# Attention into routed experts on one core: load pieces, second buffers, and the work between the two phases

## The chip, the core and the metric

The kernel runs on one core of a Trainium2 chip. The core has TensorE (PE in the profile; its weight loads are PEld), VectorE (DVE), ScalarE (ACT), GpSimd (POOL) and SyncE (SP, which here only issues transfers), and 16 DMA engines that all queues share. The metric is the device time of one execution in microseconds (us). Three runs of the kernel before took 674.9, 676.65 and 677.34 us.

## The reference, cut to what matters

The output of a decayed attention without softmax is the input of a mixture of eight experts, in which every token goes to exactly one expert and every expert takes exactly 576 of the 4608 tokens.

```python
scores = q @ k.T / sqrt(64)                       # 8 batches, 8 heads, 576 positions, 64 dims
ret = (scores * where(rel >= 0, gamma[h] ** rel, 0)) @ v
x = ret.transpose(0, 2, 1, 3).reshape(4608, 512)
flat = (x @ w_gate).flatten()                     # 4608 x 8 logits
for idx in argsort(-flat):                        # greedy: best pair first
    tok, e = idx // 8, idx % 8
    if assigned[tok] < 0 and counts[e] < 576: assigned[tok] = e; counts[e] += 1
for e in range(8):
    out[assigned == e] = relu(x[assigned == e] @ w1[e]) @ w2[e]     # 512 -> 1024 -> 512
```

## The kernel before

**Attention.** The work is cut into 16 units (4 pairs of batches times 4 pairs of heads) of 9 blocks of 128 positions. A unit needs four tiles from memory: `kin` and `qin` (transposed, 128 x 1152), `vin` (128 x 1152) and `nin` (k in rows, 128 x 1024). GpSimd scales `nin` to `ks` (`kscale2`, L568). On TensorE `A` makes the products k times q (L588), which VectorE multiplies by the decay into `am` (L593). `ST` sums the running state (L605, ScalarE scales it at L611). `XS` and `XW` add state and block parts into `pX` (L630, L640), which VectorE scales into `xT` (`scale`, L652). The constants of the decay lie in the tile `cst`, a part for each pair of heads. The loads of units 0 and 1 come in pieces (`pieces`, L549, in the order of the string that `fetch` gets). Those of later units are whole tiles (`load`, L529), issued two units ahead. `kin`, `qin` and `vin` have three buffers, `nin` has one. All go out on SyncE's queue, and each tracked transfer there waits for the one eight issues earlier.

**Rows and logits.** Every four units complete a pair of batches. `logits` and `logits2` compute its logits (L669, L682), and `rows` transposes it on VectorE into the tile `xr` (L693, one buffer, three blocks to a tile), from where four transfers (L698) write it to the table `xd` in memory. The last pair's nine blocks go over TensorE: `rows_pe` turns a block by a transpose (L711) or by a product with the identity (L709), ScalarE copies it (L715) and a transfer writes it (L716). These small pieces are also used to fill TensorE's waits in the first search (`idle`).

**Routing.** The greedy choice is a search for a threshold, digit by digit. `first_digits` cuts the ordered logits into five digits, `first_table` compares them with all digit values on VectorE, `first_table_slow` does it for columns 24 to 31 on GpSimd (L202), and `count_first_pe` counts the first digit on TensorE (L241). `search_first` then goes through the digits: a product with ones (L258) broadcasts the result, VectorE finds the digit `j` (L260) and the candidates (L268), TensorE counts them with the next table (L290) and adds the carried count (L291). `members` and `listing` turn the threshold into the 576 token numbers `idx` of expert 0.

**Experts.** `gather` fetches an expert's rows from `xd` with five indirect transfers (L953), and `transposes` turns them (L969) and splits them into a high part `xh` and a low part `xl` (L971, L972). Weights come in eight chunks of 512 KB to an expert (L923, four buffers `raw`). `conv` splits a chunk into high and low: two ScalarE copies (L937, L941), and an accumulating transfer on GpSimd's queue (L942) that gives the low part; only the first chunk's low part is made by VectorE (L939). `l1` makes 16 groups of 12 products (L998), each followed by a ReLU on ScalarE (L1002), `l2` the second layer (L1037), and `scatter` writes the rows. The search for the next expert runs on VectorE beside them. A model of time (`Mixer`) decides, when the program is built, between which products its steps stand; on the chip every engine runs its list in order.

`warm` issues products of a constant tile (L1114) whose result nobody reads.

Of the kernel before, what the change touches and what calls it, by code (L numbers as in the profile page):

```python
# [23 lines left out]
def consts_np():  # L24
# [16 lines left out]
    f = lambda a: np.ascontiguousarray(a, dtype=np.float32).reshape(128, -1)  # L41
    return np.concatenate([f(m1), f(m2), f(np.stack([e1, e1, e2], axis=2)), f(ks), f(ss)], axis=1)

# [38 lines left out]
class Route:  # L82
# [14 lines left out]
    def setup(s):  # L97
# [16 lines left out]

        s.DF, s.inc, s.sm, s.oz, s.D1 = T("DF", [5, 36], BF16), T("inc", [5], I32), T("sm", [2, 5], I32), T("oe", [43, 8], BF16), T("D1", [36], F32)
        s.oe = s.oz[:, 7:]
# [7 lines left out]
        o = [256]  # L124
# [44 lines left out]
    def first_digits(s, c0, c1):  # L169

        V = s.nc.vector
        yield from s.ordered(c0, c1)
        n = c1 - c0
        d, o = s.dg[:, :5, c0:c1], s.om[:, 1:2, c0:c1].to_broadcast([128, 5, n])
        for x, op in ((o, ALU.logical_shift_right), (d, ALU.bitwise_and)):
            V.tensor_tensor(d, x, s.sm[:, op == ALU.bitwise_and, :, None].to_broadcast([128, 5, n]), op=op)
            yield
        if c1 > 24:
            V.tensor_copy(s.D1[:, c0:c1], d[:, 1])
        V.tensor_tensor(s.DF[:, :, c0:c1], d, s.inc[:, :, None].to_broadcast([128, 5, n]), op=ALU.add)  # L180
        yield
        V.tensor_tensor(s.D2[:, :, c0:c1], d[:, 2:, :, None].to_broadcast([128, 3, n, 2]),
                        s.inc[:, 2:, None, None].to_broadcast([128, 3, n, 2]), op=ALU.add)
        yield

    def first_table(s, i, g0, g1):
        n, k = g1 - g0, widths(FIRST)[i]
        if k == 64:
# [7 lines left out]
                                  op=ALU.is_le)  # L196

    def first_table_slow(s, i, c0, c1):

        for c in range(c0, c1):  # L200
            k = widths(FIRST)[i]
            s.nc.gpsimd.tensor_scalar(s.FT[i][:, c//4, :, c % 4], s.kt[:, :k, 0], s.D1[:, c:c+1], None, op0=ALU.is_le)  # L202

# [45 lines left out]
    def search_first(s):  # L249
# [4 lines left out]
        f, cp, v, oh = s.f0, s.cp0, s.DF[:, 0], s.oh  # L254
        yield 300, 30
        for i, K in enumerate(KK):
            jp = ps.tile([128, 8], F32, name="r")
# [14 lines left out]
            oh = s.oe  # L272
            t = pool.tile([128, 36], F32, name="vl")
# [3 lines left out]
            if i == 0 and len(s.pending) > 3:  # L277
                s.pending.pop(0)()
            if s.pending:
# [6 lines left out]
            for n, (a, b) in enumerate(pieces):  # L286
                yield 200, 25*(b - a)
                for c in range(a, b, w):
                    st = s.FT[i+1][:, c:c+2].rearrange("p c k -> p (c k)") if w == 2 else s.FT[i+1][:, c//4, :, c % 4]
                    nc.tensor.matmul(cw, st, s.oz[:, c+w-1:c+w+7].rearrange("p c e -> p (c e)"), start=(c == 0), stop=False, skip_group_check=True)  # L290
            nc.tensor.matmul(cw[:, 64-8*w:72-8*w], sel.to_broadcast([128, 128]), cp, start=False, stop=True, skip_group_check=True)  # L291
            if w == 1:
# [86 lines left out]
    def members(s, p):  # L379
# [24 lines left out]
        if not p:  # L404
            s.idle("rows")
            s.idle(2)
        yield (3000 if 0 < p < E - 1 else 1550 if not p else 1900), 125
# [8 lines left out]
    def listing(s, p):  # L416
# [25 lines left out]
        if not p:  # L442
            s.idle("rows")
            s.idle(6)
        for g0, g1 in ((0, 9),) if p else ((0, 5), (5, 9)):
# [62 lines left out]
def attention(tc, nc, P, qk, vk, cst_d, wg_d, rf, xd, Lg):  # L508
    cst = P['c'].tile([128, 2*1024+3*512+64+16], F32, name="cst", tag="xg")
    W0 = cst.shape[1]  # L510
    m1 = cst[:, 0:1024].rearrange("p (h q) -> p h q", h=8)
    m2 = cst[:, 1024:2048].rearrange("p (h q) -> p h q", h=8)
    ex = cst[:, 2048:3584].rearrange("p (h j q) -> p h j q", h=4, j=3)
    ks = cst[:, 3584:3648].rearrange("p (h q) -> p h q", h=4)
    ss = cst[:, 3648:3664].rearrange("p (h q) -> p h q", h=4)
    wg = P['a'].tile([128, HP, 32], F32, name="wg")
    LD = {}
    def load(u, what, cuts=None):

        bp, hp = divmod(u, HP)  # L520
        for i in what:
            n = 1024 if i == "n" else 1152
            t = P['ld'].tile([128, n], F32, name=i + "in", bufs=dict(q=3, k=3, v=3, n=1)[i])
            src = qk[bp, hp, "qk".index(i)] if i in "qk" else vk[bp, hp, :, :1152] if i == "v" else vk[bp, hp, :, 1152:]
# [9 lines left out]
    def consts(hp):  # L534
        for a, n in ((0, 256), (2048, 384), (1024, 256)):
            if a or hp:
                part(a + n*hp, a + n*hp + n)
    load(0, "kqvn", (256, 512))
    load(1, "kqvn", (512,))

    def fetch(order):
        for x in order.split():
            if x == "c":
                part(0, 256)
                part(3584, 3664)
# [27 lines left out]
    def A(g):  # L573
# [15 lines left out]
        if j == n - 1:  # L589
            m = m2 if tail else m1  # L590
            for h in range(2):
                am = P['w'].tile([128, n, 128], F32, name=f"am{h}" + tail, bufs=2)
                nc.vector.tensor_tensor(am, PA[0][h], m[:, None, 2*hp+h, :].to_broadcast([128, n, 128]), op=ALU.mult)  # L593
                for i in range(n): AM[g-j+i, h] = am[:, i]
# [105 lines left out]

    def rows_pe(bp, blk, product=False, hps=range(HP)):

# [40 lines left out]
    for bp in range(NP):  # L743
        g0 = (bp+1)*4*NB + 2
        for k, b0 in enumerate((0, 3, 6)):
# [11 lines left out]
            else:  # L757
# [3 lines left out]
                else:  # L761
                    at(G-1, lambda it: rest(both(it, R.first_digits(27, 30))), it)
        if bp < NP-1:
# [69 lines left out]
    bp = NP-1  # L833
    left = [lambda b=b: rows_pe(bp, b, b > 0) for b in range(NB)]

# [17 lines left out]
    some(1)  # L853
    return R, [lambda b=b, h=h: rows_pe(bp, b, True, h) for b in range(NB - len(left), NB) for h in [(x,) for x in range(HP)]]

# [31 lines left out]
def moe(tc, nc, P, R, xd, w1_d, w2_d, out, mix):  # L887
# [8 lines left out]
    spacer = P['c'].tile([1, 1], F32, name="spacer")  # L896

# [78 lines left out]
    def l1(e, tr):  # L976
# [5 lines left out]
        for i, (f, s) in enumerate(order):  # L982
# [88 lines left out]
    def run():  # L1071
# [5 lines left out]
        mix.step()  # L1077
        warm(20)
        mix.adv(3500)
        tr = transposes(0)  # L1080
        next(tr)
        warm(3)
# [9 lines left out]
def build(tc, nc, qk, vk, cst, wg, rf, w1, w2, out):  # L1092
    with ExitStack() as top:
# [4 lines left out]
        top.enter_context(tc.manual_schedule())  # L1098
        xd = dr.tile([N, DM], F32, name="xd")
        it = P['c'].tile([128, 128], I32, name="it")  # L1100
        nc.gpsimd.iota(it, pattern=[[1, 128]], base=0, channel_multiplier=-1)
# [4 lines left out]
        mix = Mixer()  # L1106
        full = P['c'].tile([128, 512], BF16, name="full")
        nc.vector.memset(full, 1.0)

# [6 lines left out]
        with ExitStack() as ctx:  # L1116
# [5 lines left out]
            def idle(what):  # L1122

                if what not in ("row", "rows"):
                    warm(what)
                    return
                for _ in range(1 + (what == "rows")):
                    if rows:
                        rows.pop(0)()
                    else:  # L1130
                        warm(1)
            R.idle = idle
            run = moe(tc, nc, P, R, xd, w1, w2, out, mix)
# [23 lines left out]
```

## Time and profile before

| what | value |
|---|---|
| three runs | 674.9, 676.65, 677.34 us |
| the profiled execution: own time, span | 674.55 us, 672.8 us |
| TensorE busy | 632.0 us, 94% of the span |
| VectorE, ScalarE, GpSimd busy | 422.3, 273.6, 180.7 us |
| moved by DMA | 134.72 MB, mean 200 GB/s |
| idle TensorE up to 240 us, where attention, routing and the first layer of expert 0 lie | 27.8 us |

The span is cut into stages by time: the attention's units run up to about 174 us, the last rows and the first search up to 198 us, the gathers of expert 0 up to 207 us, and the experts from there to the end. A row of the timeline gives an instruction's start, its duration and, in brackets, how long its engine was idle before it and what it waited for. One float32 product shows as two instructions on TensorE.

### The profile page before, as it was taken

The numbers are of one execution on the slowest core, as the hardware profiler recorded it, in microseconds if no ns is written. First come the engines' busy times: TensorE is split into PE (matmuls) and PEld (weight loads), VectorE is DVE, ScalarE is ACT, GpSimd is POOL, SyncE is SP. The second block draws the span as 40 slices with busy tenths as digits, with TensorE's granted clock in tenths as the row PEclk, the third lists the DMA queues.
The fourth block names the chain that finished last, engine by engine and source line by source line (L and its number), as shares of the span: only waits on it lengthen the run. The fifth ranks groups of instructions, "written<-read, shape, count | busy, mean of one in ns | idle before, by whom it ended". The sixth has DMA issues, their size and how long they took to land.

```text
span 672.8 us, 14118 instructions
## 1 busy us (share of the span) xinstructions
PE 632.0 (94%) x5376; PEld 543.3 (81%) x5376; DVE 422.3 (63%) x1603; ACT 273.6 (41%) x488; POOL 180.7 (27%) x234
## 2 busy tenths in 40 slices
PE   4999999897987999999999999999999999999995
PEld 3887788776756887797798799889889989988984
DVE  2477878777775797798799599679776302211200
ACT  1333333232325524655257245515724643652611
POOL 2222212212212106315214323315224134131111
PEclk9999999899998999999999999999999999999998
DMA  7997999993455946978859938947894895894421
GB/s 225 340 362 251 285 306 307 257 282 91 126 198 137 227 96 203 258 192 199 247 130 230 243 81 215 245 145 172 210 245 118 177 268 177 194 237 137 94 63 39
DMA packets 53427, 134.72 MB, mean 200 GB/s; under 512 B 6128, under 2 KB 22512, under 8 KB 53360
## 3 DMA queue, kind: packets, MB, share of 16 engines
q1 hardware_dynamic: 38400, 81.91, 37.1%
q0 software_dynamic: 14960, 51.91, 35.1%
q8 instruction: 42, 0.69, 0.4%
q14 instruction: 25, 0.20, 0.1%
HBM read 81.90 MB, written 18.87 MB: 150 GB/s over the span
## 4 chain that ended last, share of the span: by engine, by line
PE 63%; DVE 12%; issue 9%; DMA 8%; POOL 3%; ACT 3%; SPq 2%; POOLq 0%; DVEq 0%; ACTq 0%
PE py L1037 21%; PE ph L998 21%; PE pX L640 4%; PE pA L588 3%; PE pX L630 3%; PE pS L605 3%; DMA w2l<-raw 2%; DMA raw<-in_w 1%; POOL xg L953 1%; DMA qin<-in_qk 1%; PE pt L969 1%; PE r L340 1%; DMA xd<-xr 1%; PE pT L669 1%; DVE xr L693 1%
## 5 line engine op out<-in xcount | busy, mean ns | idle before, releaser
L1037 PE MATMUL py<-w2h,hb 128*128 128x512 f32 x576 | 188.3, 399 | 0.0
L998 PE MATMUL ph<-xh,w1h 128*128 128x320 f32 (+1 forms) x512 | 152.6, 302 | 2.5 <-ACT xh L971 1.7
L998 PE MATMUL ph<-xh,w1l 128*128 128x320 f32 (+1 forms) x512 | 150.0, 297 | 0.0
L998 PE MATMUL ph<-xl,w1h 128*128 128x320 f32 (+1 forms) x512 | 149.9, 297 | 0.0
L1037 PE MATMUL py<-w2l,hb 128*128 128x512 f32 (+1 forms) x320 | 125.4, 392 | 0.1
L1037 PEld LDWEIGHTS py<-w2h,hb 128*128 128x128 f32 x576 | 104.0, 188 | 20.7
L998 PEld LDWEIGHTS ph<-xh,w1h 128*128 128x128 f32 x512 | 96.7, 190 | 4.7 <-ACT xh L971 2.8
L998 PEld LDWEIGHTS ph<-xl,w1h 128*128 128x128 f32 x512 | 96.9, 191 | 0.5 <-DVE cs L344 0.3
L998 PEld LDWEIGHTS ph<-xh,w1l 128*128 128x128 f32 x512 | 96.7, 191 | 0.2 <-DMA w1l<-raw 0.2
L1005 DVE SCALAR_TENSOR_TENSOR hb<-ph,hb 128x256 fp32r<-128x256 f32 (+1 forms) x192 | 58.9, 351 | 56.9 <-ACT hb L1002 56.2
L1002 ACT ACTIVATE hb<-ph 128x256 fp32r<-128x256 f32 (+1 forms) x128 | 52.2, 409 | 102.1 <-PE ph L998 102.1
L611 ACT ACTIVATE S<-pS,cst 64x128 f32<-64x128 f32 x128 | 46.4, 363 | 108.1 <-PE pS L605 106.5
L1014 POOL DMA_INDIRECT out_y<-yt,idx x40 | 40.8, 1021 | 118.8 <-ACT yt L1054 76.6
L1037 PEld LDWEIGHTS py<-w2l,hb 128*128 128x128 f32 (+1 forms) x320 | 56.7, 177 | 13.7 <-DMA w2l<-raw 1.0
L568 POOL TENSOR_TENSOR ks<-nin,cst 128x512 f32<-128x512 f32 (+1 forms) x33 | 33.3, 1028 | 120.8 <-DMA nin<-in_vk 100.9
L1054 ACT ACTIVATE yt<-py 128x512 f32<-128x512 f32 x32 | 19.2, 599 | 105.1 <-PE py L1037 78.9
L942 POOL DMA_DIRECT2D w2l<-raw x32 | 28.8, 901 | 119.2 <-ACT hb L1002 119.2
L593 DVE TENSOR_TENSOR am<-pA,cst 128x512 f32<-128x512 f32 x64 | 41.0, 682 | 27.9 <-PE pA L588 21.8
L953 POOL DMA_INDIRECT xg<-xd,idx x40 | 40.7, 1017 | 51.6 <-issue 26.6
L1057 DVE TENSOR_TENSOR yt<-yt,py 64x512 f32<-64x512 f32 x8 | 5.4, 678 | 69.6 <-ACT yt L1056 69.4
L588 PE MATMUL pA<-qin,kin 64*128 64x128 f32 x512 | 39.5, 295 | 8.6 <-DMA qin<-in_qk 8.6
L588 PEld LDWEIGHTS pA<-qin,kin 64*128 64x128 f32 x512 | 33.0, 196 | 12.8 <-issue 8.0
(190 smaller groups left out, 967.8 us busy)
## 6 DMA issues: line engine op xcount, KB each, us to landing
raw<-in_w SPq DMA_DIRECT2D x64, 512.0 KB, 5.3
w2l<-raw POOLq DMA_DIRECT2D x32, 512.0 KB, 5.7
w1l<-raw POOLq DMA_DIRECT2D x31, 512.0 KB, 7.7
kin<-in_qk SPq DMA_DIRECT2D x14, 576.0 KB, 6.3
qin<-in_qk SPq DMA_DIRECT2D x14, 576.0 KB, 7.1
vin<-in_vk SPq DMA_DIRECT2D x14, 576.0 KB, 7.9
nin<-in_vk SPq DMA_DIRECT2D x14, 512.0 KB, 5.8
xd<-xr SPq DMA_DIRECT2D x36, 192.0 KB, 3.6
```

Source lines behind the costliest of these rows:

```text
L568: nc.gpsimd.tensor_tensor(KS[u][:, a:b], LD[u, 'n'].rearrange("p (a d) -> p a d", d=64)[:, a:b], ks[:, u % HP, a:b, None].to_broadcast([12 ...
L588: nc.tensor.matmul(PA[0][h][:, j], LD[u, 'k'][r, s], LD[u, 'q'][r, s], start=True, stop=True, skip_group_check=True)
L593: nc.vector.tensor_tensor(am, PA[0][h], m[:, None, 2*hp+h, :].to_broadcast([128, n, 128]), op=ALU.mult)
L611: nc.scalar.activation(st[64*h:64*h+64, :, 64*h:64*h+64], PS[u][64*h:64*h+64], AF.Copy, scale=ss[64*h:64*h+64, hp, c:c+1])
L640: nc.tensor.matmul(px[64*h:64*h+64, :], v[:, blk*128+64*h:blk*128+64*h+64], AM[g, h], start=False, stop=blk < 8, skip_group_check=True)
L942: nc.gpsimd.dma_start(lo, raw, accum_op=ALU.add)
L953: nc.gpsimd.indirect_dma_start(out=xg[:n, j, :], out_offset=None, in_=xd[:, :], in_offset=bass.IndirectOffsetOnAxis(ap=found[e][:n, j:j+1] ...
L998: T.matmul(ps, w, x, start=(k == 0), stop=(k == 11))
L1002: A.activation(hb[:, f, c], ps, AF.Relu)
L1005: V.scalar_tensor_tensor(hb[:, f, to+a:to+b], ps[:, a:b], 0.0, hb[:, f, 256*s+a:256*s+b].bitcast(F32), op0=ALU.max, op1=ALU.subtract)
L1014: st = nc.gpsimd.indirect_dma_start(out=out[:, :], out_offset=bass.IndirectOffsetOnAxis(ap=found[e][:n, t:t+1], axis=0), in_=y[:n], in_off ...
L1037: T.matmul(ps[:m], a, w, start=(k == 0), stop=(k == last), skip_group_check=True)
```

## The change

It has four parts.

1. **Start of the attention.** The constants are laid out so that each pair of heads takes one transfer instead of three. The first pieces of unit 0 are 512 columns instead of 256 and all pieces of units 0 and 1 are issued at once; the first `qin` piece goes out on ScalarE's queue. Seven `warm` products precede the first four blocks of `A`.
2. **Second buffers.** `nin` and `xr` get two buffers.
3. **Digits and rows.** Columns 24 to 27 and 28 to 35 of the second digit's table are made by VectorE, and the six last columns get their digits in one pass. All last rows are turned by transposes, in half blocks. The carried count is added between the two parts of a count, not behind it.
4. **Late weights.** Only two chunks of expert 0 are requested before the gathers. A transfer of one element, which waits for the fourth gather, stands in SyncE's queue ahead of the others. The conversions of the first layer move to other groups, and there are more `warm` products.

On SyncE's queue the program begins as follows, before and then after (k, q, v, n are the four tiles, `cst` the constants):

```order
L549 DMA kin<-in_qk 128x256
L549 DMA qin<-in_qk 128x256
L532 DMA cst<-in_cst 128x256
L532 DMA cst<-in_cst 128x80
L549 DMA vin<-in_vk 128x256
L549 DMA nin<-in_vk 128x256
L549 DMA kin<-in_qk 128x256
L549 DMA qin<-in_qk 128x256
L532 DMA cst<-in_cst 128x384
L532 DMA cst<-in_cst 128x256
L549 DMA nin<-in_vk 128x256
L549 DMA vin<-in_vk 128x256
```

```order
L537 DMA kin<-in_qk 128x512
L523 DMA cst<-in_cst 128x336
L537 DMA nin<-in_vk 128x512
L537 DMA vin<-in_vk 128x512
L537 DMA kin<-in_qk 128x640
L537 DMA qin<-in_qk 128x640
L523 DMA cst<-in_cst 128x640
L537 DMA nin<-in_vk 128x512
L537 DMA vin<-in_vk 128x640
```

Unit 0 and its constants took sixteen transfers, of which the first twelve stand here. Now they take nine on this queue, and the first `qin` piece has left it.

On VectorE these rows stand between the last count of the first digit and the first search step (`om`, `dg`, `DF`, `D` are the digits' steps, `f` and `cp` the first digit's result, `j` the digit found), before and then after:

```order
L180 TENSOR_TENSOR DF<-dg,inc 128x5x3
L182 TENSOR_TENSOR D_496<-dg,inc 128x3x6
L246 TENSOR_TENSOR f_2301<-cnt,room_478 128x8
L247 TENSOR_TENSOR cp_2302<-cnt,room_478 128x8
L155 TENSOR_SCALAR om<-m 128x3
L157 TENSOR_TENSOR om<-m,om 128x3
L176 TENSOR_TENSOR dg<-om,sm 128x5x3
L176 TENSOR_TENSOR dg<-dg,sm 128x5x3
L179 CAST D_495<-dg 128x3
L180 TENSOR_TENSOR DF<-dg,inc 128x5x3
L182 TENSOR_TENSOR D_496<-dg,inc 128x3x6
L260 TENSOR_REDUCE j<-r 128x1
```

```order
L223 TENSOR_TENSOR G_2264<-rc_f,m 128x384
L214 TENSOR_TENSOR oh<-t_476,mx_477 128x24
L156 TENSOR_SCALAR om<-m 128x6
L158 TENSOR_TENSOR om<-m,om 128x6
L239 TENSOR_TENSOR f_2284<-cnt,room_473 128x8
L240 TENSOR_TENSOR cp_2285<-cnt,room_473 128x8
L177 TENSOR_TENSOR dg<-om,sm 128x5x6
L177 TENSOR_TENSOR dg<-dg,sm 128x5x6
L179 TENSOR_TENSOR DF<-dg,inc 128x5x6
L181 TENSOR_TENSOR D_490<-dg,inc 128x3x12
L254 TENSOR_REDUCE j<-r 128x1
```

The digits of the last six columns, which were made in two passes of seven instructions, are made in one of six.

On SyncE's queue the last row of `xd` is followed by the weights of expert 0 (`raw`), before and then after:

```order
L716 DMA xd_65<-xT_2239 128x512
L923 ISA
L923 DMA raw_2554<-in_w1 128x1024
L923 ISA
L923 DMA raw_2556<-in_w1 128x1024
L923 ISA
L923 DMA raw_2558<-in_w1 128x1024
```

```order
L701 DMA xd_65<-xT_2231 128x512
L905 ISA
L905 DMA raw_2551<-in_w1 128x1024
L905 ISA
L905 DMA raw_2553<-in_w1 128x1024
L1069 DMA spacer1_2293<-xg_2611 1x1
L905 ISA
L905 DMA raw_2695<-in_w1 128x1024
```

Behind the second chunk now stands a transfer that reads the gathered rows `xg`. On TensorE the order of all products of the experts is the one of before, and so it is on VectorE.

The diff, without the renamed lines and the `warm` counts:

```diff
-        if c1 > 24:
-            V.tensor_copy(s.D1[:, c0:c1], d[:, 1])
...
-    def first_table_slow(s, i, c0, c1):
-
-        for c in range(c0, c1):
-            k = widths(FIRST)[i]
-            s.nc.gpsimd.tensor_scalar(s.FT[i][:, c//4, :, c % 4], s.kt[:, :k, 0], s.D1[:, c:c+1], None, op0=ALU.is_le)
...
                 for c in range(a, b, w):
-                    nc.tensor.matmul(cw, st, s.oz[:, c+w-1:c+w+7].rearrange("p c e -> p (c e)"), start=(c == 0), stop=False, skip_group_check=True)
-            nc.tensor.matmul(cw[:, 64-8*w:72-8*w], sel.to_broadcast([128, 128]), cp, start=False, stop=True, skip_group_check=True)
+                    nc.tensor.matmul(cw, st, s.oz[:, c+w-1:c+w+7].rearrange("p c e -> p (c e)"), start=(c == 0), stop=(c + w == 36), skip_group_check=True)
+                if n == 0:
+                    nc.tensor.matmul(cw[:, 64-8*w:72-8*w], sel.to_broadcast([128, 128]), cp, start=False, stop=False, skip_group_check=True)
...
-            t = P['ld'].tile([128, n], F32, name=i + "in", bufs=dict(q=3, k=3, v=3, n=1)[i])
+            t = P['ld'].tile([128, n], F32, name=i + "in", bufs=dict(q=3, k=3, v=3, n=2)[i])
...
     def consts(hp):
-        for a, n in ((0, 256), (2048, 384), (1024, 256)):
-            if a or hp:
-                part(a + n*hp, a + n*hp + n)
-    load(0, "kqvn", (256, 512))
+        part(80 + 896*hp + (0 if hp else 256), 976 + 896*hp)
+    load(0, "kqvn", (512,))
...
-                part(0, 256)
-                part(3584, 3664)
+                part(0, 336)
...
-                nc.sync.dma_start(*pieces[x[0].isupper(), x[0].lower()].pop(0))
-    fetch("k0 q0 c v0 n0 k1 q1 h0 n1 v1 k2 q2 n2 v2")
+                (nc.scalar if x == "q0" else nc.sync).dma_start(*pieces[x[0].isupper(), x[0].lower()].pop(0))
+    fetch("k0 q0 c n0 v0 k1 q1 h0 n1 v1 K0 Q0 h1 N0 V0 K1 Q1 N1 V1")
...
-            TR[0] = P['w'].tile([128, 12, HP, 32], F32, name="xr", bufs=1)
+            TR[0] = P['w'].tile([128, 12, HP, 32], F32, name="xr", bufs=2)
...
-            if product:
-                nc.tensor.matmul(o, x, ident, start=True, stop=True)
-            else:
-                nc.tensor.transpose(o, x, ident)
+            nc.tensor.transpose(o, x, ident)
...
-    kscale2(0, 0, 4)
-    A(0)
-    A(1)
+    kscale2(0, 0, 8)
+    P['warm'](7)
+    for g in range(4):
+        A(g)
     ST(0, 0)
-    kscale2(0, 4, 8)
     kscale2(0, 8, 16)
-    fetch("K0 Q0 N0 V0 h1 K1 Q1 N1 V1")
-    A(2)
-    A(3)
...
-    R.first_table_slow(1, 24, 28)
-    b = R.first_digits(30, 33)
+    R.first_table(1, 6, 7)
     logits2(bp, 6, 9)
     some(3)
-    rest(both(R.count_first(33, 36), b))
-    R.first_table_slow(1, 28, 32)
-    c = R.first_digits(33, 36)
+    P['warm'](2)
+    rest(R.count_first(33, 36))
+    c = R.first_digits(30, 36)
+    for _ in range(2):
+        next(c)
     R.count_first_pe([27, 30, 33], **tag())
     rest(c)
-    R.pending = [lambda: R.first_table(1, 8, 9)] + [lambda i=i: R.first_table(i, 6, 9) for i in (2, 3, 4)]
+    R.pending = [lambda: R.first_table(1, 7, 9)] + [lambda i=i: R.first_table(i, 6, 9) for i in (2, 3, 4)]
...
-    state = dict(dma=0, conv=0, most=4, listing=-1)
+    state = dict(dma=0, conv=0, most=2, listing=-1)
...
-            if s and f in (1, 2, 4, 6) or e == 0 and i < 3:
+            if s and f in (1, 2, 4, 6) or e == 0 and i in (0, 2, 4):
                 conv()
...
         mix.adv(800)
+
+        nc.sync.dma_start(spacer2, XG[0][0:1, 3, 0:1])
         state['most'] = 8*E
+        dma_pump()
```

## Rows read from the trace of the kernel before

**Rows 1.** Windows of the start: us busy per engine (instructions), PEclk, DMA share, GB/s

```profile
2.20:28.36 26.16, 17.79 (x200) 15.52 (x201) 8.18 (x16) 6.36 (x15) 4.50 (x6) 1.00 0.88 291
14.00:16.00 2.00, 2.00 (x16) 1.75 (x12) 1.31 (x3) 0.00 (x0) 0.41 (x2) 1.00 0.40 117
16.00:28.00 12.00, 11.26 (x154) 9.89 (x152) 5.58 (x12) 4.17 (x12) 2.09 (x2) 1.00 0.95 339
36.00:46.00 10.00, 9.75 (x148) 8.49 (x146) 7.07 (x38) 3.81 (x12) 2.05 (x2) 1.00 1.03 373
```

**Rows 2.** Timeline of the start, TensorE: start, us, instruction, idle before and releaser

```profile
12.62 2.08 PE L588 MATMUL pA<-qin,kin 64*128 64x128 f32 x16 [3.56 <-DMA qin<-in_qk]
...
28.36 1.16 PE L588 MATMUL pA<-qin,kin 64*128 64x128 f32 x16 [1.02 <-DMA qin<-in_qk]
```

**Rows 3.** Waits of TensorE from 0 to 240: total us, times, longest

```profile
PE pA L588 <- DMA qin<-in_qk: 8.6, 4, 3.6
PE pX L630 <- DVE xT L652: 6.8, 4, 2.8
```

**Rows 4.** Timeline of the attention's last units, VectorE and TensorE

```profile
150.55 0.71 DVE L693 STREAM_TRANSPOSE xr<-xT 128x512 f32<-128x512 f32 x1 [1.35 <-DMA xd<-xr]
...
152.32 0.49 PE L630 MATMUL pX<-qin,S 128*128 128x128 f32 x2 [1.39 <-DVE xT L652]
...
162.68 0.71 DVE L693 STREAM_TRANSPOSE xr<-xT 128x512 f32<-128x512 f32 x1 [2.02 <-DMA xd<-xr]
...
164.22 0.49 PE L630 MATMUL pX<-qin,S 128*128 128x128 f32 x2 [2.75 <-DVE xT L652]
```

**Rows 5.** Windows behind these stalls

```profile
152.00:158.00 6.00, 5.56 (x80) 4.88 (x82) 5.22 (x16) 1.61 (x5) 2.04 (x2) 1.00 0.22 83
164.00:170.00 6.00, 5.77 (x65) 4.24 (x65) 4.89 (x12) 2.18 (x6) 0.00 (x0) 0.72 0.08 15
```

**Rows 6.** Timeline from the last logits to the third digit, VectorE and TensorE

```profile
176.90 0.25 DVE L684 TENSOR_REDUCE Lg<-pT 128x24 f32<-128x96 f32 x1
...
180.66 0.16 DVE L260 TENSOR_REDUCE j<-r 128x1 f32<-128x8 f32 x1
...
181.92 0.42 DVE L194 TENSOR_TENSOR FT<-kt,DF 128x512 bf16<-128x512 bf16 x1
...
184.74 0.55 DVE L190 TENSOR_TENSOR FT<-k,D 128x768 bf16<-128x768 bf16 x1
...
184.81 0.37 PE L291 MATMUL r<-cp,sel 128*128 128x8 f32 x2
...
185.32 0.17 DVE L299 COPY cn<-r 64x8 f32<-64x8 f32 x1
```

**Rows 7.** Chain that ended last, from the first gather to expert 0's second layer

```profile
200.66 5.39 DMA xg<-xd,idx
...
207.47 2.81 PE ph L998 x12
...
240.52 1.49 PE py L1037 x6
```

**Rows 8.** Timeline of expert 0's first pieces, GpSimd, ScalarE and TensorE

```profile
204.64 0.99 POOL L953 DMA_INDIRECT xg<-xd,idx  x1 [0.30 <-issue]
...
212.48 1.35 ACT L971 ACTIVATE xh<-pt 128x512 fp32r<-128x512 f32 x3
...
213.88 0.86 PE L998 MATMUL ph<-xh,w1h 128*128 128x320 f32 x4 [0.92 <-ACT xh L971]
```

**Rows 9.** Tile xg: time to landing of the gathers

```profile
DMA to landing us min/median/max: 3.0/3.6/6.9
```

**Rows 10.** Tile w1l: time to landing of the low weights

```profile
DMA to landing us min/median/max: 4.7/7.7/10.5
```

**Rows 11.** Windows around the gathers and behind them

```profile
198.00:203.00 5.00, 3.66 (x18) 1.47 (x15) 3.83 (x13) 1.06 (x1) 3.23 (x3) 1.00 0.97 351
207.50:210.00 2.50, 2.50 (x12) 2.50 (x13) 0.55 (x1) 0.00 (x0) 0.00 (x0) 0.50 0.03 7
```

More of the change, by code (lines that the diff above doesn't have):

```diff
@@ L41, in consts_np @@
     f = lambda a: np.ascontiguousarray(a, dtype=np.float32).reshape(128, -1)
-    return np.concatenate([f(m1), f(m2), f(np.stack([e1, e1, e2], axis=2)), f(ks), f(ss)], axis=1)
+    ex = np.stack([e1, e1, e2], axis=2)
+    return np.concatenate([f(ks), f(ss)] + [f(a) for p in range(HP) for a in (m1[:, 2*p:2*p+2], ex[:, p], m2[:, 2*p:2*p+2])], axis=1)
 def layout(q, k, v):
@@ L112, in setup @@
         s.tri, s.up = cb[:, 0], cb[:, 1]
-        s.DF, s.inc, s.sm, s.oz, s.D1 = T("DF", [5, 36], BF16), T("inc", [5], I32), T("sm", [2, 5], I32), T("oe", [43, 8], BF16), T("D1", [36], F32)
+        s.DF, s.inc, s.sm, s.oz = T("DF", [5, 36], BF16), T("inc", [5], I32), T("sm", [2, 5], I32), T("oe", [43, 8], BF16)
         s.oe = s.oz[:, 7:]
@@ L255, in search_first @@
         yield 300, 30
+        s.idle("row")
         for i, K in enumerate(KK):
@@ L272, in search_first @@
             oh = s.oe
+            if i == 0:
+                s.pending.pop(0)()
             t = pool.tile([128, 36], F32, name="vl")
@@ L276, in search_first @@
             V.tensor_tensor(v, t, s.DF[:, i+1], op=ALU.add)
-            if i == 0 and len(s.pending) > 3:
-                s.pending.pop(0)()
             if s.pending:
@@ L404, in members @@
         if not p:
-            s.idle("rows")
-            s.idle(2)
+            s.idle(6)
         yield (3000 if 0 < p < E - 1 else 1550 if not p else 1900), 125
@@ L442, in listing @@
         if not p:
-            s.idle("rows")
-            s.idle(6)
+            s.idle(9)
         for g0, g1 in ((0, 9),) if p else ((0, 5), (5, 9)):
@@ L509, in attention @@
     cst = P['c'].tile([128, 2*1024+3*512+64+16], F32, name="cst", tag="xg")
[L510 to L515, printed above, removed]
+    ks = cst[:, 0:64].rearrange("p (h q) -> p h q", h=4)
+    ss = cst[:, 64:80].rearrange("p (h q) -> p h q", h=4)
+    cq = cst[:, 80:].rearrange("p (h j q) -> p h j q", h=4, j=7)
+    m1, ex, m2 = cq[:, :, 0:2], cq[:, :, 2:5], cq[:, :, 5:7]
     wg = P['a'].tile([128, HP, 32], F32, name="wg")
@@ L589, in A @@
         if j == n - 1:
-            m = m2 if tail else m1
+            m = (m2 if tail else m1)[:, hp]
             for h in range(2):
                 am = P['w'].tile([128, n, 128], F32, name=f"am{h}" + tail, bufs=2)
-                nc.vector.tensor_tensor(am, PA[0][h], m[:, None, 2*hp+h, :].to_broadcast([128, n, 128]), op=ALU.mult)
+                nc.vector.tensor_tensor(am, PA[0][h], m[:, None, h, :].to_broadcast([128, n, 128]), op=ALU.mult)
                 for i in range(n): AM[g-j+i, h] = am[:, i]
@@ L699, in rows, with rows_pe @@
                                   TR[0][32*a:32*a+32].rearrange("p b h i -> p b (h i)"))
-    def rows_pe(bp, blk, product=False, hps=range(HP)):
+    def rows_pe(bp, blk, hps=range(HP)):
         if 0 in hps:
@@ L761, in attention @@
                 else:
-                    at(G-1, lambda it: rest(both(it, R.first_digits(27, 30))), it)
+                    at(G-1, lambda it, k: rest(both(it, R.first_digits(27, 30) if k else iter(()))), it, k)
         if bp < NP-1:
@@ L833, in attention @@
     bp = NP-1
-    left = [lambda b=b: rows_pe(bp, b, b > 0) for b in range(NB)]
+    left = [lambda b=b: rows_pe(bp, b) for b in range(NB)]
     def some(n):
@@ L842, in attention @@
     some(1)
-    R.first_table_slow(1, 24, 28)
-    b = R.first_digits(30, 33)
+    R.first_table(1, 6, 7)
     logits2(bp, 6, 9)
     some(3)
-    rest(both(R.count_first(33, 36), b))
-    R.first_table_slow(1, 28, 32)
-    c = R.first_digits(33, 36)
+    P['warm'](2)
[3 more added lines that the diff above has]
+        next(c)
     R.count_first_pe([27, 30, 33], **tag())
     rest(c)
-    R.pending = [lambda: R.first_table(1, 8, 9)] + [lambda i=i: R.first_table(i, 6, 9) for i in (2, 3, 4)]
-    some(1)
-    return R, [lambda b=b, h=h: rows_pe(bp, b, True, h) for b in range(NB - len(left), NB) for h in [(x,) for x in range(HP)]]
+    R.pending = [lambda: R.first_table(1, 7, 9)] + [lambda i=i: R.first_table(i, 6, 9) for i in (2, 3, 4)]
+    return R, [lambda b=b, h=h: rows_pe(bp, b, h) for b in range(NB - len(left), NB) for h in (range(2), range(2, HP))]
 class Mixer:
@@ L892, in moe @@
     regs, XG = {}, {}
-    state = dict(dma=0, conv=0, most=4, listing=-1)
+    state = dict(dma=0, conv=0, most=2, listing=-1)
     RAW, W1, W2, XH, XL = {}, {}, {}, {}, {}
     scat = []
-    spacer = P['c'].tile([1, 1], F32, name="spacer")
+    spacer, spacer2 = [P['c'].tile([1, 1], F32, name=f"spacer{i}") for i in range(2)]
     def phases():
@@ L1077, in run @@
         mix.step()
-        warm(20)
+        warm(25)
         mix.adv(3500)
@@ L1081, in run @@
         next(tr)
-        warm(3)
+        warm(4)
         next(tr)
@@ L1099, in build @@
         xd = dr.tile([N, DM], F32, name="xd")
+        full = P['c'].tile([128, 512], BF16, name="full")
+        nc.vector.memset(full, 1.0)
         it = P['c'].tile([128, 128], I32, name="it")
@@ L1106, in build @@
         mix = Mixer()
-        full = P['c'].tile([128, 512], BF16, name="full")
-        nc.vector.memset(full, 1.0)
         def warm(n):
@@ L1122, in idle @@
             def idle(what):
[L1124 to L1127, printed above, removed]
+                if what in ("row", "rows"):
                     if rows:
@@ L1131, in idle @@
                         warm(1)
+                    what = 2*(what == "rows")
+                if what:
+                    warm(what)
             R.idle = idle
```

## The prediction

> **What bounds the kernel now.** I read the busy shares first. TensorE is busy for 94% of the span, so a gain must lie where it waits, and the waits of TensorE up to 240 us name two places in the attention: for the q tile from memory, 8.6 us in 4 waits, and for VectorE's `xT`, 6.8 us in 4 [rows 3]. The windows of the start tell what the first wait is. From 2.2 to 28.36 us the DMA engines move 291 GB/s, with a hole of 117 GB/s from 14 to 16, while they reach 339 behind it and 373 at 36 to 46 us [rows 1]. The timeline shows TensorE stopped at 12.62 for the second piece of unit 0's q and at 28.36 for unit 2's [rows 2]: the start is a stream from memory, not work. For the second place the timeline of the last units shows VectorE idle for 1.35 and 2.02 us before a transpose into `xr`, until a transfer has read that tile, and TensorE idle for 1.39 and 2.75 us behind it [rows 4]. After the longer one the clock is granted at 0.72 of 2.4 GHz over the 6 us from 164 on [rows 5]; after the shorter it stays at 1.00 [rows 5]. The last units, the search and the first expert are read from timeline and chain below; the expert phase behind them is TensorE's and the change leaves its order alone, so what is won before it arrives at the end.
>
> **The start.** The chip must have moved what lay ahead of unit 2's q: 26.16 us by 291 GB/s is 7.6 MB. The same tiles lie ahead of it after the change. With all pieces requested at once and rows of 2 KB and more, no hole is left, and I take the rate behind the hole, 339 GB/s: 7.6 / 0.339 is 22.5 us, so unit 2 starts at 24.7 instead of 28.4, 3.7 us earlier. The ends: if only the hole is filled, (339 - 117) x 2 / 339 is 1.3; with 373 GB/s it is 5.8. TensorE's own work up to there fits: 17.8 us busy, part of it at half speed. The seven warm products lie in front of the first data and cost nothing, since TensorE waits there anyway; so does the q piece on ScalarE's queue, which is empty at that time. Fewer, larger constants only take places from SyncE's queue.
>
> The Trainium skill ("DMA: Bandwidth & Descriptors", Specifications) puts the limit of memory for one core at about 358 GB/s. The row at 36 to 46 us is above it, so here it does not bind; by it this term would be 4.9 and the sum 12.7.
>
> **The second buffers.** With a second `xr` VectorE's two waits go, 1.35 + 2.02 us, and TensorE follows VectorE there. Behind them the second stall leaves TensorE 0.7 us of waiting, less than the 1.39 after which the clock stayed. So I also count the slow stretch, 6 us x (1 - 0.72) = 1.7 us, as TensorE is 5.8 us busy in it. That is 5.0 us. The low end is 3.4 with the clock falling all the same, the high end 1.39 + 2.75 + 1.7 = 5.8. A buffer adds no work, so nothing below. The second `nin` buffer takes GpSimd out of SyncE's queue; no wait of TensorE hangs on it after the start, so its worth is in the first term.
>
> **Digits, rows and the carried count.** Between the last logits' reduction at 176.90 and the first digit found at 180.66 VectorE runs 24 instructions in 3.76 us, 0.16 each, without a gap [rows 6]. Now it is 16, 1.25 us less. The table made on VectorE before them costs 0.42 us, the price of a 512-wide one [rows 6]. Net 0.8. TensorE's half as many products for the rows give nothing by themselves, since it waits for VectorE there. Moving the carried count (0.37 us) ahead of the second part also gives next to nothing: in the first three steps VectorE's table of 0.55 us ends as that product does, and the next read follows at once [rows 6]. In the first step the table is now twice as wide, which takes another 0.4 of VectorE's time, in step with TensorE's 36 products. Ends: 0, where that table ends last, and 1.6, where it hides and the four counts give 0.1 each. The rows in half blocks put 2 transposes and 2 warm products where 4 products stood; both lie in waits for VectorE.
>
> **Late weights.** In the chain the second gather takes 5.39 us to land [rows 7], against a median of 3.6 and a least of 3.0 over all [rows 9], at 351 GB/s in all [rows 11]. Two chunks (1 MB) less in that stretch let me take 3.3: the first group of the first layer starts 2.1 us earlier. It took 2.81 us for 12 products [rows 7] at a clock of 0.50 [rows 11]. With 25 and 4 warm products TensorE has no gap left before it, so it takes 1.4 and ends 3.5 us earlier. The last gather, issued at 204.64 [rows 8], lands by 208, in time for ScalarE, which first converts a chunk and then makes the three `xh` that TensorE waits for at 213.88 [rows 8]. So that point also moves by 3.5.
>
> Against it stands the price of lateness. Three chunks now go out behind the fourth gather: 1.6 MB, 4.5 us at 351 GB/s, in a stretch in which DMA was 0.03 busy [rows 11]. They fit there, but they now run beside the low part of the second weight chunk, which TensorE needs in the fifth group. That transfer lands after 4.7 us at best, 7.7 in the median, 10.5 at most [rows 10]; the empty stretch gave it the best. I charge half of the 3.0 up to the median: 3.5 - 1.5 = 2.0. The ends are 3.5 - 5.8 = -2.3, and 4.7 with gathers of 3.0 and the wait of 0.92 gone too.
>
> The Trainium skill has a rule on how queues share an engine ("DMA: Bandwidth & Descriptors", Queues, rings and completion order): each engine goes round its queues by packets. By it a gather beside the chunks loses only half of the rate: 0.26 MB at 176 instead of 351 GB/s, 0.75 us instead of 2.1, and the sum would be 10.1. The landing of 5.39 against 3.0 says that it loses more here.
>
> **Sum.** 3.7 + 5.0 + 0.8 + 2.0 = 11.5 us; all low ends give 1.3 + 3.4 + 0 - 2.3 = 2.4, all high ends 5.8 + 5.8 + 1.6 + 4.7 = 17.9. The profiled execution took 674.55 us, its span 672.8. It is quicker than the three runs; the median of all four is 675.8, and from there the forecast is 664.3 us.
>
> **Rivals.**
> - *Forecast*, a gain of 9 to 15 us, 661 to 667: 0.55.
> - *Less*: the stream stays as slow as in the first pieces and weights are late: 1.3 + 5.0 + 0.8 - 2.3 = 4.8, 671.0 us. For it speaks that outside the hole, too, the start averages only (7613 - 234) KB / 24.16 us = 305 GB/s, against it that its pieces get larger. 0.20.
> - *More*: every high end, 657.9 us. For it speaks that single stretches move 373 GB/s; against it that a stream over 20 us does not hold its best rate. 0.17.
> - *The change does not do what it says*: the `xr` wait goes but the clock falls, DMA stays the limit, weights are late; all low ends, 673.4 us, which is no change (0.5%, 3.4 us, is about what a measurement can tell). 0.04.
> - *Slower*: late weights stop TensorE in expert 0's first layer, and the clock falls with the stops as it did after 164 us. The layer runs from 213.88 [rows 8] to 240.52 [rows 7], 26.6 us; half of it at half speed costs 13.3, the wait itself 5.8. Against gains of 9.5 and 3.5 elsewhere that is 675.8 - 13.0 + 19.1 = 681.9 us. It decides once more than 13 us are lost there. Against it: DMA was idle just where the chunks go now. 0.04.
>
> The range reaches from all high ends to the *less* case, 657.5 to 671. Faster by over 0.5%: 0.55 + 0.20 + 0.17 = 0.92; within it 0.04; slower 0.04.
>
> **What would show it.** Unit 2's first products at 24 to 25 us, without a window under 200 GB/s before; no wait of a transpose for an `xd` transfer, and a clock of 1.00 from 150 to 175 us; 16 instructions in about 2.6 us before the first digit; the first group of expert 0 at full clock, 12 products in about 1.4 us, its gathers landing in under 4 us; a wait of at most 2 us for the second chunk's low part. The prediction is wrong if the start gains under 2 us, or if the first layer of expert 0 gets longer by more than the gathers gain.

## The result and the profile after

The changed kernel takes 669.85 us in the median of 6 runs, the kernel before 676.25 beside it: ratio 0.9909 [0.9886, 0.9932], 6.1 us less. A second comparison, with the last experiments, gave 0.9919 [0.9892, 0.9947]. The forecast was 664.3 us, so the direction came out, and 5.5 us of the gain did not. The 669.85 us lie inside the stated range of 657.5 to 671, near its slow end, and outside the band of 661 to 667 that the prediction held likeliest. The profiled execution after took 669.9 us, its span is 668.1.

Windows of the changed kernel, with the columns of [rows 1]:

```profile
2.20:28.36 26.16, 23.44 (x272) 19.30 (x272) 10.10 (x20) 7.66 (x19) 6.35 (x7) 0.87 1.02 390
14.00:16.00 2.00, 2.00 (x30) 1.89 (x28) 0.56 (x1) 0.59 (x3) 1.04 (x1) 0.69 1.04 395
16.00:28.00 12.00, 11.92 (x178) 10.56 (x174) 6.49 (x12) 4.11 (x12) 3.08 (x3) 1.00 1.03 409
```

The hole is gone and the stream moves 390 GB/s instead of 291. The timeline of TensorE answers to [rows 2]:

```profile
8.97 2.08 PE L576 MATMUL pA<-qin,kin 64*128 64x128 f32 x16 [1.54 <-DMA qin<-in_qk]
...
23.61 1.16 PE L576 MATMUL pA<-qin,kin 64*128 64x128 f32 x16
```

Unit 2 starts at 23.61 instead of 28.36, and it no longer waits for its q. Sixteen such products take 1.16 us there and 2.08 at 8.97: in the windows of 2 us from 8 to 16 us the clock is granted at 0.50 to 0.69. In the kernel before they took 2.08 us at 12.62, too [rows 2], so that its start was slow as well, although its window there says 1.00 [rows 1].

Waits of TensorE from 0 to 240 us, which answer to [rows 3], and windows of the attention's end, which answer to [rows 5]:

```profile
PE ph L980 <- DMA w1l<-raw: 3.4, 1, 3.4
PE pX L618 <- DVE xT L640: 2.3, 3, 1.0
PE pA L576 <- DMA qin<-in_qk: 1.7, 2, 1.5
```

```profile
150.00:156.00 6.00, 5.19 (x74) 4.20 (x71) 5.82 (x19) 2.09 (x6) 0.00 (x0) 1.00 0.55 125
156.00:162.00 6.00, 5.17 (x64) 3.14 (x66) 3.98 (x12) 1.94 (x5) 0.00 (x0) 1.00 0.41 89
162.00:168.00 6.00, 5.05 (x58) 4.15 (x60) 5.54 (x33) 3.21 (x7) 0.00 (x0) 1.00 0.40 127
```

The waits for q and `xT` have shrunk and the clock holds at 1.00. But the first line is new. The chain of waits, which answers to [rows 7], has the same transfer, and the timeline of TensorE shows it:

```profile
189.83 3.55 DMA xg<-xd,idx
...
194.71 1.72 PE ph L980 x12
...
199.03 8.41 DMA w1l<-raw
```

```profile
203.77 0.28 PE L980 MATMUL ph<-xl,w1h 128*128 128x256 f32 x1
207.49 0.58 PE L980 MATMUL ph<-xh,w1l 128*128 128x256 f32 x1 [3.45 <-DMA w1l<-raw]
207.88 0.42 PE L980 MATMUL ph<-xh,w1h 128*128 128x256 f32 x1
```

```profile
199.00:203.80 4.80, 4.01 (x28) 3.81 (x27) 4.42 (x19) 2.96 (x7) 0.98 (x1) 1.00 0.92 271
203.80:207.50 3.70, 0.25 (x4) 0.05 (x2) 0.86 (x4) 2.83 (x4) 1.45 (x2) 0.85 1.01 210
207.50:210.00 2.50, 2.50 (x18) 2.40 (x19) 0.30 (x2) 0.00 (x0) 0.28 (x1) 0.50 1.05 187
210.00:213.20 3.20, 3.20 (x15) 3.20 (x14) 2.91 (x12) 2.28 (x3) 0.14 (x1) 0.50 1.04 256
```

The low part of chunk 1 is issued at 199.03, beside the three raw chunks issued from 197.10 on, and lands after 8.41 us, which is inside the range of [rows 10]. The fifth group waits 3.45 us for it, and behind the wait the clock is at half speed for 5.7 us more.

The lead over the kernel before in us, read at the same instructions of the two timelines (where nothing else is said, at the start of what is named), tells where it is won and lost:

```
unit 1           3.65      end of unit 15    11.18    3rd group, expert 0   13.86
units 3 and 4    4.97      last logits       11.18    expert 0, layer 2      8.41
units 8 to 11    5.03      first digit's     12.02    expert 4, layer 1      8.47
unit 12          6.85        products                 expert 4, layer 2      5.57
unit 15          7.92      first gather's    12.1     end                    4.65
                             transpose
```

13.86 us are won before expert 0's third group, 5.4 are lost in that layer and 2.9 in expert 4's first layer. Not all of what is won is the change's. The 1.8 us between units 11 and 12 come from a stop of the kernel before that has no `xr` transfer in it, and from the slow clock behind it (the same stop is 1.00 us after the change):

```profile
121.02 0.53 PE L630 MATMUL pX<-qin,S 128*128 128x128 f32 x2 [1.68 <-DVE xT L652]
```

Its clock is at 0.56 from 121 to 124 us. In a second profile of the same kernel (`e9_before_again`) the stop is 0.82 us and the clock stays at 1.00.

### The profile page after: what moved, and what is told of

Its sections match the earlier page's. It is cut to its first block, busy times and chain, and to the rows that moved or that the text cites. A ratio compares the mean times of both kernels' runs of the same rounds, so it can differ in the third digit from the quotient of the medians.

```text
span 668.1 us, 14067 instructions
## 1 busy us (share of the span) xinstructions
PE 632.6 (95%) x5368; PEld 539.2 (81%) x5372; DVE 420.8 (63%) x1594; ACT 272.6 (41%) x488; POOL 176.4 (26%) x225
## 4 chain that ended last, share of the span: by engine, by line
PE 65%; DVE 12%; issue 9%; DMA 8%; ACT 2%; POOL 2%; SPq 1%; POOLq 0%; ACTq 0%; DVEq 0%
PE py L1019 23%; PE ph L980 20%; PE pA L576 4%; PE pX L628 4%; PE pX L618 3%; PE pS L593 3%; DMA w2l<-raw 2%; DMA raw<-in_w 2%; PE r L335 2%; PE pt L951 2%; DMA nin<-in_vk 1%; PE pT L657 1%; DMA w1l<-raw 1%; PE pX L616 1%; DVE G L168 1%
## 5 line engine op out<-in xcount | busy, mean ns | idle before, releaser
L556 POOL TENSOR_TENSOR ks<-nin,cst 128x512 f32<-128x512 f32 x32 | 33.7, 1071 | 113.2 <-DMA nin<-in_vk 94.4
L924 POOL DMA_DIRECT2D w1l<-raw x31 | 27.6, 902 | 57.2 <-ACT w1l L923 42.7
```

What stands on the lines that cost most here:

```text
L556: nc.gpsimd.tensor_tensor(KS[u][:, a:b], LD[u, 'n'].rearrange("p (a d) -> p a d", d=64)[:, a:b], ks[:, u % HP, a:b, None].to_broadcast([12 ...
L924: nc.gpsimd.dma_start(lo, raw, accum_op=ALU.add)
```

## Experiments: the late weights

**Chunk 1's low part on VectorE** (`e1_low_on_vector`), in place of the accumulating transfer:

```diff
         conv(True)
+        conv(True)
         mix.step()
...
-            if s and f in (1, 2, 4, 6) or e == 0 and i in (0, 2, 4):
+            if s and f in (1, 2, 4, 6) or e == 0 and i in (2, 4):
```

> Chunk 1's low part is made by ScalarE and VectorE right behind chunk 0's, so no accumulating transfer stands before the fifth product group. Theory L (the missing gain is that one wait and the slow clock behind it, because the accumulate of chunk 1 ran beside three raw chunks): the 3.45 us wait goes and the clock stays at 1.00 from 200 to 215 us; first product to first output product of expert 0 takes about 32 us instead of 37.25; time 669.9 - 5 = 664.5 to 665.5 us. Rival R (DMA is simply short in that stretch): the wait reappears at the ninth group for chunk 2, the layer takes 35 us or more, time 668 us or above.

664.53 us, ratio 0.9829 [0.9796, 0.9862]. The wait is gone, the layer takes 32.26 us, as theory L had it. It is not shorter because a new wait follows. Timeline of TensorE, and windows:

```profile
215.77 0.39 PE L335 MATMUL r<-oh,G 128*128 128x32 bf16 x9 [1.79 <-DVE G L168]
```

```profile
203.00:214.00 11.00, 10.98 (x96) 10.57 (x94) 6.58 (x30) 9.61 (x14) 3.56 (x4) 1.00 0.88 222
214.00:222.00 8.00, 6.23 (x49) 6.13 (x50) 6.48 (x27) 3.15 (x5) 0.85 (x1) 0.79 1.06 249
```

ScalarE is busy for 9.61 of 11 us with four conversions in a row, the relus and with them VectorE's search come late, and behind the wait the clock falls, to 0.79 in the mean of 8 us.

**Conversions spread out** (`e5_spread`), on top of that:

```diff
-            if s and f in (1, 2, 4, 6) or e == 0 and i in (2, 4):
+            if s and (f in (1, 2, 4, 6) or e == 0 and f in (3, 5)):
```

> As e1_low_on_vector, and the six conversions left in expert 0's first layer stand at every second product group instead of four in a row. Theory A (in e1 four conversions in a row keep ScalarE from the relus from 203 to 213 us, VectorE's search digit comes late by them, TensorE waits 1.79 us at 215.8 and the clock falls behind it): that wait is under 0.5 us, no clock below 1.00 at 215 to 222 us, first product to first output product under 30.5 us instead of 32.26; time 661 to 662.5 us. Rival D (VectorE's own chain of the search sets it): the wait stays, 664 to 665 us.

663.32 us, ratio 0.9823 [0.9787, 0.9858]. In the trace theory A holds: no wait for `G` in that layer, layer 29.38 us, no slow clock there. The time is above theory A's 661 to 662.5 and cannot be told from that of `e1_low_on_vector`; its runs go from 661.4 to 668.8.

**Weights as before** (`e2_weights_before`):

```diff
-    state = dict(dma=0, conv=0, most=2, listing=-1)
+    state = dict(dma=0, conv=0, most=4, listing=-1)
...
-        nc.sync.dma_start(spacer2, XG[0][0:1, 3, 0:1])
         state['most'] = 8*E
-        dma_pump()
```

> The changed kernel with the weights of expert 0 requested before the rows are gathered, as in the kernel before; all else changed. Theory L (late weights cost more than the faster gathers give): the gathers land in over 4 us again and the first product comes about 2 us later than the 194.7 of the changed kernel, but the layer takes about 33 us; the gain of 12.0 us that stood at the listing stays, time 666 to 667 us. Rival G (late weights are worth having, the loss is elsewhere): 671 to 672 us.

668.24 us, ratio 0.9895 [0.986, 0.9931]: 1 to 1.6 us better than the change (0.9909 and 0.9919), on the side of theory L though above its 666 to 667, but inside the intervals. The second gather lands after 4.83 us, as expected. The lead at the listing is not the expected 12.0 us but 8.4 in this profile, in which the clock is at half speed for 6.83 us from 76 us on, where no other profile has that. So only stretches of this profile are compared below, not its whole. The reverse, **late weights alone** (`e7_before_late`, the same lines put into the kernel before):

> The kernel before with the late weights and nothing else. Theory L (their price is the wait for chunk 1's low part and the slow clock behind it, 5.4 us, against 1.8 us from the faster gathers and the full clock of the first group): 675.3 + 1 to 3.6 = 676 to 679 us, first product to first output product 36 to 37 us instead of 33.0. Rival G (a gain, as forecast, 2.0 us): 673 us. If ScalarE's pause in expert 4 comes with them, 2.9 us more.

677.26 us, ratio 1.0004 [0.9984, 1.0024]: 0.3 us more by the ratio, so not rival G's gain of 2.0, and short of theory L's 1 to 3.6. The traces are sharper than the times. Read from the timelines, in us (means, with the range in brackets):

```
                           idx to first ph     first ph to first py   wait for w1l
weights early (6 profiles) 9.94 (9.29-11.17)   32.96 (31.82-34.05)    none
weights late (5 profiles)  9.13 (8.92-9.20)    35.70 (33.99-37.25)    3.0 to 3.8
e1_low_on_vector           9.29                32.26                  none
e5_spread                  9.22                29.38                  none
```

The late weights bring the first product 0.8 us forward, and the layer then takes 2.7 us more: a net loss of 1.9 us. (The two groups mix kernels that differ in other parts, so these are rough.) The wait is in all five profiles, the fall of the clock behind it in four.

The gathers do land sooner, the second after 3.55 us instead of 5.39. What takes most of that back is GpSimd, which issues them. Timeline of its first gather, before and then after:

```profile
199.16 1.19 POOL L953 DMA_INDIRECT xg<-xd,idx  x1 [18.41 <-DMA raw<-in_w]
```

```profile
187.50 2.03 POOL L935 DMA_INDIRECT xg<-xd,idx  x1 [38.40 <-ACT w1h L919]
```

It starts 1.33 us behind the last instruction on `idx` instead of 0.95, and takes 0.84 us longer, so the second gather goes out 1.2 us later. Why is not shown: eight of the fourteen profiles have a first gather of 1.92 to 2.18 us, among them `e8_digits_alone` with its weights early.

## Experiments: start, second buffer, digits

**One `xr` buffer** (`e3_one_xr`: `bufs=2` back to `bufs=1`), and the **second buffer alone** (`e6_before_two_xr`: the kernel before with `bufs=2`):

> The changed kernel with one xr buffer. Theory B (the second buffer is the 6 us that came between units 11 and 16, its clock included): both waits of VectorE for the xd transfer return, the clock falls behind the second and at about 121 us, time 669.9 + 5 to 6 = 675 to 676 us. Rival C (the waits alone, the clock keeps): 669.9 + 3.4 = 673 us. Rival N (those units were sped up by the earlier transfers of the start): 670 us.

> The kernel before with a second xr buffer and nothing else. Theory B (the buffer alone is worth what e3 lost, 5 to 6 us, as the clock no longer falls behind the waits): 669.5 to 670.5 us, no wait of VectorE for the xd transfer, clock 1.00 from 150 to 175 us. Rival C (only the two waits, 3.4 us): 672 us. If ScalarE's pause in expert 4's first layer comes with the moved buffers, that layer takes 31.5 us here, too, instead of 28.6, and the time is 2.9 us more than either.

674.79 us, ratio 0.9996 [0.9976, 1.0017], and 671.25 us, ratio 0.9927 [0.9901, 0.9953]. Without the buffer 5.2 to 5.9 us are lost (0.9996 against 0.9919 and 0.9909), with it alone 4.9 are won. In `e3_one_xr` VectorE waits 1.35, 1.28 and 1.75 us for the `xd` transfer and the clock is at half speed for 3.41 us from 157.09 on, but not at 121 us, as theory B had it. In `e6_before_two_xr` there is no such wait, and the clock is 1.00 from 150 to 175 us. So the traces are on the side of theory B. The time of the second, 671.25 us, lies between those of B and of rival C and does not decide between them.

**Start as before** (`e4_start_before`), and the **start alone** in the kernel before (`e10_start_alone`):

```diff
-    fetch("k0 q0 c n0 v0 k1 q1 h0 n1 v1 K0 Q0 h1 N0 V0 K1 Q1 N1 V1")
+    fetch("k0 q0 c v0 n0 k1 q1 h0 n1 v1 k2 q2 n2 v2")
...
-    P['warm'](7)
-    for g in range(4):
-        A(g)
+    A(0)
+    A(1)
```

> The changed kernel with the start of the kernel before: small pieces, one nin buffer, no warm products, unit 1's second pieces late. Theory S (the stream is the limit and unit 2 starts when its q has landed): a hole in the DMA rate at 14 to 16 us, unit 2's first products at 28 us instead of 23.6, time 669.9 + 4.8 = 674 to 675 us. Rival A (later waits absorb part of an earlier start): 671 to 673 us.

> The kernel before with the larger first pieces, q on ScalarE's queue, two nin buffers and the warm products; constants as before. Theory S (the start is worth what e4 lost, 4 to 5 us): 671.5 to 672.5 us, unit 2 at 24 us. Rival A (the start's gain is partly lost where the kernel waits later, at the xr transfers): 673 to 675 us with the wait of VectorE for xr longer than the 1.35 and 2.02 us of before.

673.54 us, ratio 0.9969 [0.9945, 0.9994], and 673.11 us, ratio 0.9953 [0.9927, 0.9978]: the start is worth 3.4 to 4.1 us in company and 3.2 alone. Neither run moves the constants: the first keeps their new layout, the second the old one, so what their fewer transfers are worth is in neither number. Unit 2 starts at 26.67 and at 24.42 us. Over all profiles it starts at 26.27 to 28.36 with the old start (six) and at 21.55 to 24.42 with the new one (eight); the profile that the forecast was made from has the latest of all. Rival A's place is there as well: VectorE's waits for `xr` in `e10_start_alone` are 1.34, 1.66 and 1.91 us. The last two stand against 1.35 and 2.02 in [rows 4], the first has no counterpart there, and the clock falls twice, at 149 and at 163 us. That may take back part of the gain; no run tests it.

**Digits, rows and carried count alone** (`e8_digits_alone`: start, `xr` and weights as before):

> The changed kernel with the start, the single xr buffer and the weights of the kernel before: what is left of the change are the digits at once, the rows as transposes and the carried count. Theory C (worth 0.8 us and nothing else): 674.5 us, expert 4's first layer takes 28.6 us. Rival P (ScalarE's pause in expert 4 comes with this part): that layer takes 31.5 us, 677 us.

675.89 us, ratio 0.9988 [0.9967, 1.001]: 0.8 us, as theory C had it, but not told from none (the new layout of the constants is in it, too). Expert 4's first layer takes 31.5 us, the pause of rival P; the section on the pause tells whose it is. In the whole change the timeline of VectorE answers to [rows 6]:

```profile
166.03 0.25 DVE L672 TENSOR_REDUCE Lg<-pT 128x24 f32<-128x96 f32 x1
...
168.80 0.16 DVE L254 TENSOR_REDUCE j<-r 128x1 f32<-128x8 f32 x1
```

**Clock at the start** (`e11_spread_warm`, on top of `e5_spread`), with the **changed kernel again** beside it (`e12_after_again`):

```diff
     for g in range(4):
         A(g)
+        if g == 1:
+            P['warm'](10)
```

> As e5_spread with ten warm products between the first and the second pair of A groups. Theory K (the slow clock from 8 to 16 us in some executions delays the start by up to 2 us once the data are in time): clock 1.00 from 6 to 16 us, 661.5 to 662.5 us. Rival Q (the start ends with the stream all the same): 663 to 664 us.

> The changed kernel, unchanged, beside the kernels above on one chip. Both theories of the weights expect a ratio of 0.991 to the kernel before; if the wait for chunk 1's low part is its lasting price, it is there again with 3 to 4 us, and e11_spread_warm is 5 us or more faster.

662.35 us, ratio 0.9803 [0.9774, 0.9832], against 669.34 us for the changed kernel: the lowest median of all, 7.0 us below the change, and its six runs lie within 2.1 us. The windows of its start:

```profile
6.00:8.00 2.00, 2.00 (x16) 1.01 (x13) 0.00 (x0) 0.00 (x0) 0.67 (x1) 1.00 1.04 409
8.00:10.00 2.00, 1.49 (x22) 1.06 (x19) 1.29 (x2) 1.34 (x2) 0.58 (x1) 1.00 1.05 397
10.00:12.00 2.00, 2.00 (x32) 1.76 (x30) 1.46 (x4) 0.67 (x2) 0.61 (x2) 1.00 1.05 398
```

The clock stays at 1.00 and unit 2 starts at 21.60, 2.0 us earlier than in the first profile of the change. In `e5_spread` the clock happened to hold in the profiled execution, and unit 2 started at 21.55 behind a wait of 0.93 us for q. It held in the second profile of the changed kernel, too, and there unit 2 again waits for its q:

```profile
21.57 1.16 PE L576 MATMUL pA<-qin,kin 64*128 64x128 f32 x16 [0.52 <-DMA qin<-in_qk]
```

So 21.6 us is where the stream ends: 7.6 MB at 390 GB/s are 19.5 us from 2.2 on. The same program is 2 us later in its first profile, where the clock has fallen. The ratios of the two kernels differ by 0.002 with overlapping intervals, so the gain in time is not shown.

## Experiment: the pause in expert 4

The 2.9 us lost in expert 4's first layer have no wait behind them. There ScalarE starts a relu late, and TensorE stops, too. All profiles up to here except that of the kernel before have this, also with only `xr` changed. **The kernel before, profiled again** (`e9_before_again`):

> The kernel before, unchanged, with a second profile. Theory M (ScalarE's pause in expert 4's first layer comes and goes between executions and is not the change's): that layer takes 31.5 us here, too, and the experts from first product to last output product take 461 us instead of 458.07. Theory Z (the pause comes with any change of the kernel): 28.6 and 458 us.

678.35 us, one run. Timeline of ScalarE in it:

```profile
457.17 0.38 ACT L1002 ACTIVATE hb<-ph 128x256 fp32r<-128x256 f32 x1 [0.88 <-PE ph L998]
462.23 0.44 ACT L1002 ACTIVATE hb<-ph 128x320 fp32r<-128x320 f32 x1 [4.67 <-PE r L340]
```

Timelines of TensorE and GpSimd at that place:

```profile
462.16 0.31 PE L998 MATMUL ph<-xh,w1l 128*128 128x320 f32 x1 [0.85 <-issue]
```

```profile
461.26 1.03 POOL L942 DMA_DIRECT2D w2l<-raw  x1
```

The same two relus in the first profile of the kernel before:

```profile
458.09 0.39 ACT L1002 ACTIVATE hb<-ph 128x256 fp32r<-128x256 f32 x1 [0.66 <-PE ph L998]
459.85 0.44 ACT L1002 ACTIVATE hb<-ph 128x320 fp32r<-128x320 f32 x1 [1.37 <-PE ph L998]
```

The layer takes 33.00 us here, 28.57 there, the experts 464.5 instead of 458.07. Theory M holds: the pause is not the change's. (The 33.00 us are more than its 31.5, as the clock falls to half speed here for 3.41 us at 469 us.) The profile from which the sum was made lacked the pause by chance, so the lead table above overstates the loss by it. What stops ScalarE was not found. TensorE stops in the middle of a product group with nothing to wait for (`issue`) and goes on 0.07 us before ScalarE, so it does not wait for the relu. In all thirteen profiles that have it, the pause ends within 0.1 us of the time at which GpSimd has issued the first accumulating transfer behind five gathers (here 461.26 + 1.03 us). Whether the one causes the other was not tried; in the profile without a pause ScalarE does not wait for that transfer.

## Why the forecast came out too high, step by step

- *The start* (3.7 us): right, 3.2 to 4.1 in time, but partly by luck. The mechanism is the one named. The rate was higher than taken, 390 instead of 339 GB/s, and held over the whole stream, which the prediction doubted under its rival *more*. By its own sum, 7.6 MB at that rate would give 6.7 us; TensorE's work at half speed, which it took to fit in, kept 2 of them in the profile of the change. The limit of about 358 GB/s, which the Trainium skill gives ("DMA: Bandwidth & Descriptors", Specifications), is exceeded here: 390 over 26 us.
- *The second buffers* (5.0 us): right, 4.9 alone and 5.2 to 5.9 in company. That is more than the two waits (3.4), so the slow clock was part of the price, as the term had it.
- *Digits, rows, carried count* (0.8 us): right as far as can be told, 0.84 us in the lead table (11.18 to 12.02), 0.8 in time. From the last logits' reduction to the first digit VectorE takes 2.77 us instead of 3.76.
- *Late weights* (2.0 us): wrong, in size and in sign, a loss of 1.9 us in the profiles and of 0.3 to 1.6 in time, which is not clear of noise. Two of its terms were mis-sized. First, "the first group of the first layer starts 2.1 us earlier": it was 0.8. The second gather did land 1.84 us sooner, but GpSimd issued it 1.2 us later, a term that the prediction does not have. With the first group at full clock (1.72 us instead of 2.81) the third group came 1.8 us forward (12.02 to 13.86), not 3.5. By the rule on queues that the prediction weighed and set aside (the Trainium skill, "DMA: Bandwidth & Descriptors", Queues, rings and completion order) the landing would have gained 0.75 us. The 1.84 are nearer to the prediction's own 2.1, so the 0.8 us to the first product do not speak for that rule: GpSimd's delay made them. Second, "I charge half of the 3.0 up to the median": the transfer took 8.41 us, the wait was 3.0 to 3.8 us, and a slow clock came behind it in four profiles of five. The prediction took its landing from a stretch without raw chunks; the change itself put three of them beside it. It had named this collision, but had the clock's fall behind such a stop only in a rival. The signs by which the prediction itself was to be judged (a wait of at most 2 us for that part; the layer no longer by more than the gathers gain) show it wrong here.

By the parts alone the change should bring 3.2 + 4.9 + 0.8 - 0.3 = 8.6 us; it brings 5.5 to 6.1. The intervals of the single terms are 1.4 to 1.8 us on either side, so it is open whether the 2.5 to 3.1 us between them are more than the errors of the four terms together.

Of the rivals, *less* (671.0 us) was the nearest: its weights were late as it said, its start was not slow.

## What to carry to other kernels

When transfers are moved out of one wait, price the transfers that are issued next to their new place, with the collision in them: the landing time read from a stretch without other weights, 4.7 us, became 8.41 here. A small conversion that an engine with room does itself can be worth more than a better order of transfers: it gave 5.4 to 6.1 us here (0.9829 against 0.9909 and 0.9919). Before a difference between two profiles is explained, profile the unchanged kernel a second time.

## What the runs showed of the hardware

The clock decides on many small terms. Five profiles have the stop for chunk 1. In these, a longer stop goes with more slow clock behind it, and the layers with more slow clock are the longer ones (us):

```
                   stop    half speed behind it    layer
e12_after_again    2.97    none                    33.99
e3_one_xr          3.07    3.4                     34.99
e4_start_before    3.24    3.4                     35.23
after              3.45    5.7                     37.25
e7_before_late     3.79    5.8                     37.04
```

Windows of `e12_after_again`, whose wait of 2.97 us ends at 206.56:

```profile
200.00:206.00 6.00, 3.60 (x25) 3.39 (x24) 4.08 (x21) 4.36 (x6) 0.87 (x1) 1.00 0.96 279
206.00:212.00 6.00, 5.44 (x53) 5.29 (x54) 3.70 (x16) 3.72 (x6) 1.70 (x2) 1.00 1.04 224
```

The clock is 1.00 on both sides of the stop, so stops that differ by 0.5 us go with layers that differ by 3.3 (2.97 and 3.45 us). ScalarE pauses for 4 to 4.7 us at one place of the program in thirteen profiles out of fourteen, and TensorE for 0.4 to 1 us with it, without a wait that the trace shows.
